# The order of the last loads and of the last products in a one-core decode kernel (attention, gated feed-forward, mixed)

## The chip, the cores and the metric

One core of a Trainium2 chip. The metric is the device time of one execution in microseconds, the median of several runs. Unless marked ns, all times are microseconds from the start of the span.

## The reference

One token `x` of 512 numbers goes through two branches, and a gate mixes them:

```python
q = (x @ wq) as 32 heads of 128          # D = 512
# 8 key heads of 32768 x 128, each shared by 4 query heads
p = softmax(q . k * 128**-0.5)
a = concat_heads(p @ v) @ wo             # wo: 4096 x 512
b = (silu(x @ w1) * (x @ w3)) @ w2       # w1, w3: 512 x 1792, w2: 1792 x 512
g = sigmoid(sum(x * gate_w))
out = g * a + (1 - g) * b                # 512 numbers
```

All is float32. In units of 2^20 bytes, keys and values are 128 MB each, wo and wq 8 MB each, w1, w3 and w2 3.5 MB each; each byte is read once, 296.2 million bytes in all.

## The kernel before, in words

The kernel writes out the order of each engine by hand: a small planner (`Program`) keeps a list of operations per engine and puts a semaphore wait wherever an operation reads or overwrites what another engine or a transfer has written. Nothing is reordered after that. All large loads are issued by SP (`load`, whose DMA is line 191), in the order in which they stand in the program; a load that has to wait for its buffer holds back every load behind it.

Two large buffers of 8 MB, `big_a` and `big_b`, take keys and values. Each has two halves of 4 MB, `region(b, z)`, whose keys in the planner are A0, A1, B0, B1. In the main part, keys come through `big_a` (two early tiles through `big_b`), VectorE transposes them in 32 x 32 blocks, TensorE forms the scores, and values of earlier heads come through `big_b` and are multiplied by the probabilities. The keys of all eight heads and the values of heads 0 to 5 go through this; the part runs to about 600 us.

The end of the kernel, lines 478 to 649, is written out straight:

- `load_halves` and further loads bring the last values, heads 6 and 7 (half-heads 12 to 15), each in one or more pieces. `values` (line 540) multiplies one half buffer, or some of its four groups of 16 blocks, and accumulates in the bank `ps_o`.
- `load_wo(w)` loads a quarter of wo (2 MB) into the one buffer `wo_t`. `mix(w)` (line 527) adds the rows of that quarter on VectorE, eight additions into `acc` [128 partitions x 512], weighted with the attention outputs of heads 2w and 2w + 1. The loads of quarters 1 to 3 therefore each wait for the eighth addition of the quarter before. The fourth quarter isn't mixed on VectorE: its products run on TensorE.
- `last_head(h)` (lines 549 to 556) takes a head's sum out of `ps_o` by four VectorE operations, a product on TensorE (line 555), and a scaling; `place` (lines 509 to 521) spreads the result over the partitions by a multiplication, a product (line 513), a mask and a sum. For the last head the result is `otp`, the weights of the last wo products.
- w2 goes into `region(0, 0)`, 14 row blocks `k` of 512 columns (`w2t[:, k, :]`), in five transfers `parts`: blocks 0 to 3, 4 to 7, 8 to 10, 11 and 12, 13.
- `wide` (line 624) multiplies by blocks 0 to 7 of w2 and by the last wo and accumulates into bank f0 (`pa`) in four groups of 32 partitions. VectorE then adds `pa` to `acc` (line 632). `ff_down` (line 639) accumulates into bank f1 (`pb`): first `ones` times `acc`, the sum over the partitions, then blocks 8 to 13 of w2. `res` is the copy of `pb` (line 647), and ScalarE's queue issues the output.
- `idle_product(n)` (line 606) is a product of n columns whose result nobody reads. It waits for nothing; TensorE, which takes its instructions in order, does it where it stands.

The order of the last loads on SP before: third wo; B0; B1a (2 MB); the wait for `mix(2)`; fourth wo; B1b and B1c (1 MB each); the five parts of w2. The order of TensorE before, from the last values on: values of B0, B1a, B1b; idle 512; values of B1c; idle 512 and 256; last head; `place`; w2 blocks 0 to 3; idle 256; wo; w2 blocks 4 to 7; (VectorE's addition, beside it idle 512); sum of `acc` over partitions; w2 blocks 8 to 13.

A float32 product is two records in the profile, so that "x16" under line 540 or 624 is eight products.

Of the kernel before, what the change touches and what calls it, by code (L numbers as in the profile page):

```python
# [116 lines left out]
def kernel(  # L117
# [14 lines left out]
    _, HKV, S, DH = k_cache.shape  # L132
# [12 lines left out]
    R = NB * DH  # L145
# [3 lines left out]
    FR = F // P  # L149
# [11 lines left out]
    def sbuf(name, *shape):  # L161
        return nc.alloc_sbuf_tensor(name, [P, *shape], F32)[:]

    big = [sbuf("big_a", 2 * R), sbuf("big_b", 2 * R)]
    wo_t = sbuf("wo_t", 8, D)
# [11 lines left out]
    acc = sbuf("acc", 512)  # L177
    otp = sbuf("otp", 8, 32)
    htp = sbuf("htp", FR, 32)
# [7 lines left out]
    def load(dst, src, writes, over=()):  # L187
        lanes[0] += 1
        lane = f"load{lanes[0] % 12}"
        return pr.add(  # L190
            "SP", lambda: nc.sync.dma_start(dst, src), writes=writes, over=[*over, lane], inc=lane, by=16, also=lane,
        )

    def region(b, z):
        return big[b][:, z * R:(z + 1) * R]
# [12 lines left out]
    ident, ones, fold = sbuf("ident", P), sbuf("ones", P), sbuf("fold", 32)  # L208
# [18 lines left out]
    for src, dst, view, axes in (  # L227
# [11 lines left out]
            reads=[src], writes=[dst])  # L239
# [24 lines left out]
    for c in range(NC):  # L264
# [19 lines left out]
        reads=["gate0"], writes=["gate1"])  # L284
# [41 lines left out]
    vd = v_cache.rearrange("a h (e p n) d -> (a h) e p (n d)", e=2, p=P)  # L326
# [155 lines left out]
    def load_wo(w):  # L482
        load(wo_t, wo[w * 8 * P:(w + 1) * 8 * P, :].rearrange("(p k) e -> p k e", k=8), ["wo"])
# [22 lines left out]
    def place(ws, rows, i, over=()):  # L506
        n, w0 = len(ws), ws[0]
        mine = each[i][:, 0:n]
        dve(lambda: V.tensor_mul(
            mine, on[:, 8 * w0:8 * w0 + 8 * n].rearrange("p (w t) -> p w t", w=n).unsqueeze(2).to_broadcast([P, n, 8, 8]),  # L510
            own_k.unsqueeze(1).unsqueeze(3).to_broadcast([P, n, 8, 8]),
        ), reads=["own_k"] + [("on", 2 * w + u) for w in ws for u in range(2)], writes=[f"each{i}"])
        pe(lambda: T.matmul(  # L513
            pm[i][:, 0:64 * n], spot.rearrange("p t x -> p (t x)"), mine.rearrange("p w k t -> p (w k t)"),
            start=True, stop=True,
        ), reads=["spot", f"each{i}"], writes=[f"m{i}"])
        dve(lambda: V.tensor_mul(
            mine, pm[i][:, 0:64 * n].rearrange("p (w k t) -> p w k t", w=n, t=8),
            mask.unsqueeze(1).unsqueeze(1).to_broadcast([P, n, 8, 8]),
        ), reads=[f"m{i}", "mask"], writes=[f"each{i}"])  # L520
        dve(lambda: V.tensor_reduce(rows, mine, axis=AX.X, op=ALU.add),
            reads=[f"each{i}", *over], writes=[("own", w) for w in ws])


    def mix(w):
        for k in range(8):
            dve(lambda k=k: V.scalar_tensor_tensor(  # L527
                acc, wo_t[:, k, :], own_rows[:, w, k:k + 1], acc, op0=ALU.mult, op1=ALU.add,
            ), reads=["wo", ("own", w), "acc"], writes=["acc"])


    def values(h, e, z, vt, key, groups=range(4)):
        u = h % 2

        def go():
            for g in groups:
                for t in range(4):
                    o = 256 * g + 128 * z + 64 * e + 16 * t
                    n = 16 * g + 4 * t
                    ins = T.matmul(  # L540
                        ps_o[32 * t:32 * t + 32, :], prob[u][:, o:o + 32], vt[:, n * P:(n + 4) * P],
                        start=((e, z, g) == (0, 0, 0)), stop=((e, z, g) == (1, 1, 3)),
                    )
            return ins
        pe(go, reads=[key, f"pad{u}", ("prob", u)], writes=["o"])

    def last_head(h):
        r = red[h % 2]
        dve(lambda: V.tensor_scalar(r, ps_o[:, 0:P], own_b[:, 0:1], None, op0=ALU.mult),  # L549
            reads=["o", "own_b"], writes=[("red", h % 2)])  # L550
        for b in range(1, 4):
            dve(lambda b=b: V.scalar_tensor_tensor(
                r, ps_o[:, b * P:(b + 1) * P], own_b[:, b:b + 1], r, op0=ALU.mult, op1=ALU.add,
            ), reads=["o", "own_b", ("red", h % 2)], writes=[("red", h % 2)])
        pe(lambda: T.matmul(pm[1][:, 0:REP], r, own_q, start=True, stop=True), reads=["own_q", ("red", h % 2)], writes=["m1"])
        dve(lambda: V.tensor_mul(on[:, 4 * h:4 * h + 4], pm[1][:, 0:REP], recip[:, 4 * h:4 * h + 4]),
            reads=["m1", ("recip", 3)], writes=[("on", h)])
# [20 lines left out]
    for z in range(2):  # L578
        values(6, 1, z, region(1, z), f"B{z}")
    last_head(6)  # L580
    cuts = (0, R, R + 4096, R + 6144, 2 * R)
    names = ("B0", "B1a", "B1b", "B1c")

    def load_piece(i):
        a, b = cuts[i:i + 2]
        load(big[1][:, a:b], vd[7, 1][:, a:b], [names[i]], over=["B1"] if i else [])

    load_piece(0)
    load_piece(1)
    mix(2)  # L590
    load_wo(3)
    load_piece(2)
    load_piece(3)
    for z in range(2):
        values(7, 0, z, region(0, z), f"A{z}")

# [1 line left out]
    w2t = region(0, 0)[:, 0:FR * D].rearrange("p (k e) -> p k e", k=FR)  # L598
    w2d = w2.rearrange("(p k) e -> p k e", k=FR)
    parts = ((0, 4), (4, 8), (8, 11), (11, 13), (13, 14))  # L600
# [4 lines left out]
    def idle_product(n):  # L605
        pe(lambda: T.matmul(ps_s[:, 0:n], ones, sb[:, 0:4].rearrange("p n i m -> p (n i m)")[:, 0:n], start=True, stop=True),  # L606
           reads=["ones"], writes=["s"])

    values(7, 1, 0, region(1, 0), "B0")
    for n, gs in zip(names[1:], (range(0, 2), range(2, 3), range(3, 4))):  # L610
        if n == "B1c":
            idle_product(512)
        values(7, 1, 1, region(1, 1), n, gs)
    idle_product(512)
    idle_product(256)
    last_head(7)
    place(range(3, 4), otp[:, :, 0].unsqueeze(1), 1, ["otp"])
    pa, pb = pf[0], pf[1]

    def wide(ws, **kw):  # L620
        def go():
            for j, (w, t, first, last) in enumerate(ws):
                r = 32 * (j % 4)
                ins = T.matmul(pa[r:r + 32, :], w, t, start=first, stop=last)  # L624
            return ins
        pe(go, writes=["f0"], **kw)

    wide([(htp[:, k, :], w2t[:, k, :], True, False) for k in range(4)], reads=["htp", ("w2", 0)])
    idle_product(256)
    wide([(otp[:, k, :], wo_t[:, k, :], False, False) for k in range(8)], reads=[("own", 3), "otp", "wo"])  # L630
    wide([(htp[:, k, :], w2t[:, k, :], False, True) for k in range(4, 8)], reads=["htp", ("w2", 4)])
    dve(lambda: V.tensor_add(acc, acc, pa), reads=["acc", "f0"], writes=["acc"])
    idle_product(512)

    def ff_down(ws, **kw):
        def go():
            for w, t, first, last in ws:
                for j in range(4):
                    ins = T.matmul(pb[32 * j:32 * j + 32, 0:P], w, t[:, j * P:(j + 1) * P], start=first, stop=last)  # L639
            return ins  # L640
        pe(go, writes=["f1"], **kw)

    ff_down([(ones[:, 0:32], acc, True, False)], reads=["ones", "acc"])
    for a, b in parts[2:]:
        ff_down([(htp[:, k, :], w2t[:, k, :], False, k == FR - 1) for k in range(a, b)], reads=["htp", ("w2", a)])
    res = sbuf("res", P)
    dve(lambda: V.tensor_copy(res, pb[:, 0:P]), reads=["f1"], writes=["res"])
    pr.add("ACT", lambda: nc.scalar.dma_start(out.rearrange("a b (j e) -> (a b j) e", e=P), res[0:P:32, :]),
           reads=["res"], inc="out", by=16)
# [5 lines left out]
    a = next(i for i, o in enumerate(ops) if o.loop)  # L655
    b = max(i for i, o in enumerate(ops) if o.loop) + 1
# [58 lines left out]
```

## Time and profile before

| | |
|---|---|
| median of 3 runs | 699.58 us (699.52 to 699.82) |
| the profiled execution | 699.89 us |
| its span | 698.1 us |
| bytes read | 296.23 MB, 424 GB/s over the span |
| busy: TensorE, VectorE, ScalarE, GpSimd | 402.4, 376.1, 45.3, 2.6 us |
| mean granted clock of TensorE | 0.78 |

The profile gives, for each engine, the instructions with start and duration; for each transfer the time of its issue on SP and the time until it has landed; and a chain of work that ended last, followed back from the last instruction through what released each step. "PE" is TensorE, "PEld" its loading of weights, "DVE" VectorE, "SPq" the queue that SP issues transfers to. A piece of the chain that is named DMA is time in which the next step waited for that transfer. The clock of TensorE is given as a share of full speed.

### The profile page before, as it was taken

How to read it: one execution, taken by the hardware profiler on the slowest of the kernel's cores; microseconds unless marked ns; L12 is line 12 of the kernel's file. 1: busy time of each engine (PE TensorE's matmuls, PEld its weight loads, DVE VectorE, ACT ScalarE, POOL GpSimd, SP SyncE). 2: the span in 40 equal slices, each digit the busy share in tenths (PEclk: the TensorE clock that was granted, in tenths of full speed). 3: DMA queues.
4: the chain of work that ended last, by engine and by line, in shares of the span. 5: the costliest groups of instructions: out<-in, count | busy, mean ns of one | idle time of the engine just before them, and what ended most of it. 6: DMA issues, size and time to landing. Idle time of an engine off the chain costs nothing. (4 is left out here: it accounts for less than half of the span.)

```text
span 698.1 us, 5677 instructions
## 1 busy us (share of the span) xinstructions
PE 402.4 (58%) x2400; PEld 94.3 (14%) x2400; DVE 376.1 (54%) x263; ACT 45.3 (6%) x90; POOL 2.6 (0%) x15
## 2 busy tenths in 40 slices
PE   3636556656556654647565555656365565267447
PEld 1100101201010101201010101201010101121012
DVE  1029999796619091786528090886437180744301
ACT  0200000011100000020100000020001000100000
POOL 1000000000000000000000000000000000000000
PEclk9866888877887887867667886869877678676768
DMA  9999999999999999999999999999999999999994
GB/s 385 428 430 434 424 441 430 447 419 425 456 411 453 417 432 432 454 407 441 428 432 454 407 441 422 456 412 449 419 428 460 407 449 419 435 419 437 428 419 193
DMA packets 9524, 296.34 MB, mean 425 GB/s; under 512 B 1062, under 2 KB 1066, under 8 KB 1452
## 3 DMA queue, kind: packets, MB, share of 16 engines
q1 hardware_dynamic: 9506, 296.23, 98.6%
q8 instruction: 5, 0.08, 0.0%
q14 instruction: 3, 0.02, 0.0%
q10 hardware_dynamic: 10, 0.00, 0.0%
HBM read 296.23 MB, written 0.00 MB: 424 GB/s over the span
## 5 line engine op out<-in xcount | busy, mean ns | idle before, releaser
L355 DVE STREAM_TRANSPOSE kt<-big_a 128x2048 f32<-128x2048 f32 x112 | 250.3, 2287 | 182.6 <-DMA big_a<-in_A_k_cache_dram 158.4
L344 PE MATMUL ps<-kt,winc 128*32 128x512 f32 x1024 | 183.0, 795 | 132.1 <-PEq L665 131.9
L430 PE MATMUL ps<-big_b,pv 128*32 128x512 f32 x768 | 111.2, 744 | 74.3 <-PEq L665 74.3
L344 PEld LDWEIGHTS ps<-kt,winc 128*32 128x32 f32 x1024 | 26.6, 122 | 284.3 <-issue 284.3
L430 PEld LDWEIGHTS ps<-big_b,pv 128*32 128x32 f32 x768 | 30.6, 133 | 154.6 <-issue 154.6
L355 DVE STREAM_TRANSPOSE kt<-big_b 128x2048 f32<-128x2048 f32 x16 | 35.6, 2283 | 3.3 <-DMA big_b<-in_A_k_cache_dram 2.3
L244 PE MATMUL ps<-acc 128*128 128x512 f32 x34 | 22.2, 740 | 21.8 <-PEq L665 20.2
L527 DVE SCALAR_TENSOR_TENSOR acc<-wo_t,own_rows,acc 128x512 f32<-128x512 f32 x24 | 18.0, 752 | 28.5 <-DMA wo_t<-in_A_wo_dram 27.8
L540 PE MATMUL ps<-big_b,probs 128*32 128x512 f32 x128 | 20.3, 791 | 20.4 <-DMA big_b<-in_A_v_cache_dram 20.4
L338 ACT COPY winc<-win 128x128 f32<-128x128 f32 x32 | 9.8, 306 | 338.3 <-PE ps L344 338.2
L361 ACT COPY sb<-ps 128x512 f32<-128x512 f32 x16 | 17.0, 1063 | 152.9 <-PE ps L344 152.9
L540 PE MATMUL ps<-big_a,probs 128*32 128x512 f32 x128 | 19.2, 759 | 5.5 <-DMA big_a<-in_A_v_cache_dram 5.5
L403 DVE TENSOR_REDUCE sums<-probs 128x8 f32<-128x2048 f32 x4 | 15.3, 3815 | 8.0 <-ACT probs L398 8.0
L442 DVE TENSOR_TENSOR tmp<-ps,own_b 128x512 f32<-128x512 f32 x12 | 7.9, 656 | 19.8 <-PE ps L430 19.8
L307 PE MATMUL turned<-big_b,xp 128*32 128x448 f32 x64 | 10.5, 826 | 8.2 <-DMA big_b<-in_B_w_dram 8.2
L270 PE MATMUL turned<-big_a,xp 128*32 128x512 f32 x64 | 11.2, 861 | 3.1 <-DMA big_a<-in_A_wq_dram 2.9
L549 DVE TENSOR_SCALAR red<-ps,own_b 128x128 f32<-128x128 f32 x2 | 0.7, 348 | 21.3 <-PE ps L540 21.3
L446 DVE TENSOR_REDUCE red<-tmp 128x128 f32<-128x1024 f32 x6 | 11.5, 1917 | 0.2
L244 PEld LDWEIGHTS ps<-acc 128*128 128x128 f32 x34 | 5.7, 210 | 38.3 <-issue 36.7
L398 ACT ACTIVATE probs<-turned 128x1024 f32<-128x1024 f32 x8 | 7.8, 1020 | 38.5 <-DVE turned L393 38.5
L393 DVE TENSOR_TENSOR turned<-turned,top 128x2048 f32<-128x2048 f32 x4 | 9.2, 2300 | 0.1
L540 PEld LDWEIGHTS ps<-big_b,probs 128*32 128x32 f32 x128 | 4.4, 137 | 35.9 <-DMA big_b<-in_A_v_cache_dram 23.8
(80 smaller groups left out, 102.2 us busy)
## 6 DMA issues: line engine op xcount, KB each, us to landing
big_a<-in_A_k_cache_dram SPq DMA_DIRECT2D x28, 4096.0 KB, 28.5
big_b<-in_A_k_cache_dram SPq DMA_DIRECT2D x4, 4096.0 KB, 30.9
big_a<-in_A_v_cache_dram SPq DMA_DIRECT2D x4, 4096.0 KB, 28.0
big_a<-in_A_wq_dram SPq DMA_DIRECT2D x2, 4096.0 KB, 16.6
wo_t<-in_A_wo_dram SPq DMA_DIRECT2D x4, 2048.0 KB, 15.6
big_b<-in_B_w_dram SPq DMA_DIRECT2D x2, 3584.0 KB, 33.8
big_b<-in_A_v_cache_dram SPq DMA_DIRECT2D x1, 4096.0 KB, 27.3
big_b<-in_A_v_cache_dram SPq DMA_DIRECT2D x1, 2048.0 KB, 31.8
```

Source lines behind the costliest of these rows:

```text
L244: return T.matmul(ps_s, acc[:, 0:P], acc, start=True, stop=False, skip_group_check=True)
L270: ins = T.matmul(pf[b][32 * j:32 * j + 32, :], xp[:, c, :], t[:, o:o + REP * DH], start=(c == 0), stop=(c == NC - 1),)
L307: ins = T.matmul(pf[2 + z][32 * j:32 * j + 32, 0:FJ], xp[:, c, :], t[:, o:o + FJ], start=(c == 0), stop=(c == NC - 1),)
L338: lambda: A.copy(winc, win[:, t // 4, :, 16 - 16 * z:48 - 16 * z]),
L344: ins = T.matmul(ps_s[32 * g:32 * g + 32, :], winc[:, c, :], kt[c % 2][:, 512 * g:512 * g + 512], start=False, stop=False, skip_group_chec ...
L355: k = dve(lambda c=c, d=dst: V.transpose(d, kin[:, c]), reads=[key], writes=[f"kt{c % 2}"], credit="keys")
L361: lambda: A.copy(sb[:, :, :, t % 4], ps_s.rearrange("p (n i) -> p n i", i=32)),
L403: dve(lambda: V.tensor_reduce(sums[:, 8 * w:8 * w + 8].rearrange("p (u q) -> p u q", u=2), probs[:, :, 0:1024].rearrange("p u (n q) -> p u ...
L430: ins = T.matmul(ps_o[32 * t:32 * t + 32, :], pv[:, o:o + 32], big[1][:, n * P:(n + 4) * P], start=((z, g) == (0, 0)), stop=((z, g) == (1, ...
L446: dve(lambda: V.tensor_reduce(red[h], tmp.rearrange("p e b d -> p d (e b)"), axis=AX.X, op=ALU.add), reads=["tmp0", "tmp1"], writes=[("red ...
L527: dve(lambda k=k: V.scalar_tensor_tensor(acc, wo_t[:, k, :], own_rows[:, w, k:k + 1], acc, op0=ALU.mult, op1=ALU.add,), reads=["wo", ("own ...
L540: ins = T.matmul(ps_o[32 * t:32 * t + 32, :], prob[u][:, o:o + 32], vt[:, n * P:(n + 4) * P], start=((e, z, g) == (0, 0, 0)), stop=((e, z, ...
```

## The change

On SP, the second half of B1 is one transfer of 2 MB in place of two of 1 MB, and is issued directly behind B1a; the fourth wo comes behind it, and then w2 as before. The values of head 7 so come in three pieces (B0, B1a, B1b), and the fourth wo behind all of them.

On TensorE, the order from the last values on is: values of B0, B1a; idle 512 twice; values of B1b (two groups); idle 512; the last head's product, with an idle 256 between it and `place`; wo, which now starts the accumulation in `pa`; idle 512; w2 blocks 0 to 3 and 4 to 7; then, in `pb`, w2 blocks 8 to 10; the sum of `acc` over partitions; blocks 11 and 12; block 13. So the sum over partitions stands behind eleven row blocks of w2 instead of eight.

```diff
-    cuts = (0, R, R + 4096, R + 6144, 2 * R)
-    names = ("B0", "B1a", "B1b", "B1c")
-
-    def load_piece(i):
-        a, b = cuts[i:i + 2]
-        load(big[1][:, a:b], vd[7, 1][:, a:b], [names[i]], over=["B1"] if i else [])
-
-    load_piece(0)
-    load_piece(1)
+    cuts = (0, R, R + 4096, 2 * R)
+    names = ("B0", "B1a", "B1b")
+    for (a, b), n in zip(zip(cuts, cuts[1:]), names):
+        load(big[1][:, a:b], vd[7, 1][:, a:b], [n], over=[] if n == "B0" else ["B1"])
     mix(2)
     load_wo(3)
-    load_piece(2)
-    load_piece(3)
     for z in range(2):
         values(7, 0, z, region(0, z), f"A{z}")
...
     values(7, 1, 0, region(1, 0), "B0")
-    for n, gs in zip(names[1:], (range(0, 2), range(2, 3), range(3, 4))):
-        if n == "B1c":
-            idle_product(512)
-        values(7, 1, 1, region(1, 1), n, gs)
+    values(7, 1, 1, region(1, 1), "B1a", range(2))
+    for _ in range(2):
+        idle_product(512)
+    values(7, 1, 1, region(1, 1), "B1b", range(2, 4))
     idle_product(512)
+    last_head(7)
     idle_product(256)
-    last_head(7)
     place(range(3, 4), otp[:, :, 0].unsqueeze(1), 1, ["otp"])
...
-    wide([(htp[:, k, :], w2t[:, k, :], True, False) for k in range(4)], reads=["htp", ("w2", 0)])
-    idle_product(256)
-    wide([(otp[:, k, :], wo_t[:, k, :], False, False) for k in range(8)], reads=[("own", 3), "otp", "wo"])
-    wide([(htp[:, k, :], w2t[:, k, :], False, True) for k in range(4, 8)], reads=["htp", ("w2", 4)])
+    wide([(otp[:, k, :], wo_t[:, k, :], k < 4, False) for k in range(8)], reads=[("own", 3), "otp", "wo"])
+    idle_product(512)
+    for a, b in parts[:2]:
+        wide([(htp[:, k, :], w2t[:, k, :], False, k >= 4) for k in range(a, b)], reads=["htp", ("w2", a)])
     dve(lambda: V.tensor_add(acc, acc, pa), reads=["acc", "f0"], writes=["acc"])
-    idle_product(512)
...
-    ff_down([(ones[:, 0:32], acc, True, False)], reads=["ones", "acc"])
     for a, b in parts[2:]:
-        ff_down([(htp[:, k, :], w2t[:, k, :], False, k == FR - 1) for k in range(a, b)], reads=["htp", ("w2", a)])
+        ff_down([(htp[:, k, :], w2t[:, k, :], k == 8, k == FR - 1) for k in range(a, b)], reads=["htp", ("w2", a)])
+        if a == 8:
+            ff_down([(ones[:, 0:32], acc, False, False)], reads=["ones", "acc"])
```

In the changed kernel the lines behind the loads stand seven lines earlier, up to nine at the end: the products of `wide` are line 617, of `ff_down` line 631, the idle products line 599, VectorE's addition line 625, the copy to `res` line 640.

## The prediction

> **What bounds the kernel now.** I read the page first (span, slices, queues), then the chain that ended last, then SP's timeline and the list of DMA issues in the last 60 us, and last the TensorE clock by windows.
>
> ```profile
> span 698.1 us, 5677 instructions
> DMA  9999999999999999999999999999999999999994
> ```
>
> The DMA engines are full in 39 of 40 slices and not in the last: up to there the stream from memory sets the time, behind it something else does. The chain, from the last transfer in it to the last instruction that computes:
>
> ```profile
> 664.02 15.28 DMA big_b<-in_A_v_cache_dram
> 679.30 0.04 issue
> 679.35 1.94 PE ps L540 x8
> 681.28 2.00 PE ps L606 x2
> 683.29 1.63 PE ps L540 x8
> ...
> 686.51 0.40 PE ps L555 x2
> ...
> 687.41 0.43 PE ps L513 x2
> 687.84 0.99 PE turned L624 x8
> 688.84 0.63 PE ps L606 x2
> 689.47 2.71 PE turned L624 x24
> 692.18 1.06 PE ps L606 x2
> 693.23 1.71 PE turned L639 x56
> 694.97 0.29 DVE res L647
> ```
>
> From the landing of the value piece B1b at 679.30 on, the chain is TensorE and VectorE alone: the last value products, the last head, the wo products (L624), the w2 products (L624 and L639), the result. No w2 transfer is in it. Were they there long before? SP's timeline (start, duration) and the DMA issues by group (count, size, us from issue to landing; a landing below is issue plus that figure):
>
> ```profile
> 639.33 0.33 SPq L191 DMA_DIRECT2D wo_t<-in_A_wo_dram  x1
> 639.70 0.91 SPq L191 DMA_DIRECT2D big_b<-in_A_v_cache_dram  x2
> 663.65 0.33 SPq L191 DMA_DIRECT2D wo_t<-in_A_wo_dram  x1
> 664.97 2.65 SPq L191 DMA_DIRECT2D big_a<-in_B_w_dram  x5
> ```
>
> ```profile
> big_b<-in_A_v_cache_dram SPq DMA_DIRECT2D x1, 4096.0 KB, 27.3
> big_b<-in_A_v_cache_dram SPq DMA_DIRECT2D x1, 2048.0 KB, 31.8
> wo_t<-in_A_wo_dram SPq DMA_DIRECT2D x1, 2048.0 KB, 13.2
> big_a<-in_B_w_dram SPq DMA_DIRECT2D x2, 1024.0 KB, 20.3
> big_a<-in_B_w_dram SPq DMA_DIRECT2D x1, 768.0 KB, 22.7
> big_a<-in_B_w_dram SPq DMA_DIRECT2D x1, 512.0 KB, 23.5
> big_a<-in_B_w_dram SPq DMA_DIRECT2D x1, 256.0 KB, 23.6
> ```
>
> ```profile
> L191 SPq DMA_DIRECT2D big_a<-in_B_w_dram x1: 752/752/752, 666.9 to 666.9; - x1
> ```
>
> So B0 lands at 639.70 + 27.3 = 667.0, B1a at 640.2 + 31.8 = 672.0, the last wo at 663.65 + 13.2 = 676.85, B1b at 679.30; the first two w2 pieces at 665.2 + 20.3 = 685.5 on average, 1 MB apart, so 684.3 and 686.7; the next three, issued at about 665.9, 666.4 and 666.9, at 688.6, 689.9 and 690.5. They land in the order of issue, and 2 MB of distance is 4.85 us each time: one stream, served in turn. It is done at 690.5, and the result is copied out at 694.97. That gap of 4.5 us is all that a change of the end can win.
>
> **The change part by part.** *The order of the loads.* The second half of B1 (2 MB) goes out as one transfer right behind B1a, at about 640.6, and no longer behind the last wo. It needs the same buffer as B1a, so it brings no wait of its own; SP has nothing else to do until 663.65, where the eighth addition of the third wo frees wo_t. The third wo is issued ahead of all these (639.33), so that time stays. The last wo is issued at 663.65 as before, 13 us ahead of its place in the stream, and the five w2 loads queue behind it on SP, now 0.95 us earlier; neither matters while the stream serves in turn. What changes is that place: B1b takes that of the last wo (676.85), and wo takes that of B1b and B1c, 4.9 us later, at 681.75. Every w2 piece has the same bytes ahead of it, so its landing stays: the last at 690.5. One transfer less to start and to complete is worth nothing here, at least not more than the scatter of the times before (0.3 us).
>
> *The values.* The price of 16 records at full clock, of a DVE hand-over, and of a short group, by the timeline:
>
> ```profile
> 667.09 7.17 PE L540 MATMUL ps<-big_b,probs 128*32 128x512 f32 x48 [9.27 <-DMA big_b<-in_A_v_cache_dram]
> ```
>
> ```profile
> 671.98 0.12 PEld L540 LDWEIGHTS ps<-big_b,probs 128*32 128x32 f32 x4 [0.35 <-DMA big_b<-in_A_v_cache_dram]
> ```
>
> ```profile
> 688.14 0.22 DVE L521 TENSOR_REDUCE otp<-each 128x8 f32<-128x64 f32 x1
> 692.25 0.69 DVE L632 TENSOR_TENSOR acc<-acc,turned 128x512 f32<-128x512 f32 x1 [3.89 <-PE turned L624]
> ```
>
> ```profile
> 693.16 0.43 PE L639 MATMUL turned<-acc,ones 128*32 128x128 f32 x8
> ```
>
> B1a's 16 records run from 671.98 to 674.26, 2.28 us. Two idle products of 512 columns (1.06 each, as at 692.18) follow, to 676.4; then a pause of 0.5 us until B1b is there. Does the clock survive that? The windows (last three figures: granted clock, DMA share, GB/s):
>
> ```profile
> 667.00:670.00 3.00, 2.91 (x16) 0.79 (x20) 0.00 (x0) 0.00 (x0) 0.00 (x0) 0.50 1.00 426
> 671.00:674.50 3.50, 3.26 (x32) 0.73 (x24) 0.00 (x0) 0.00 (x0) 0.00 (x0) 1.00 0.95 405
> 674.50:679.30 4.80, 0.00 (x0) 0.00 (x0) 0.00 (x0) 0.00 (x0) 0.00 (x0) 0.82 1.01 418
> 679.30:684.00 4.70, 4.65 (x14) 0.91 (x18) 0.00 (x0) 0.00 (x0) 0.00 (x0) 0.50 1.01 422
> 685.00:688.00 3.00, 2.33 (x12) 1.23 (x15) 1.86 (x7) 0.00 (x0) 0.00 (x0) 1.00 1.00 406
> 690.00:690.50 0.50, 0.50 (x12) 0.13 (x4) 0.00 (x0) 0.00 (x0) 0.00 (x0) 1.00 0.00 0
> ```
>
> In the pause of 4.8 us the clock was still full for most of the time (mean 0.82), and then half for the 4.7 us behind it, which is why 8 records cost 1.94 and an idle product 2.00 in the chain. A pause of a tenth of that should keep it: I take full clock, and keep the half-clock price for the range. So the values end at 676.9 + 2.3 = 679.2, where before they ended at 684.92 (the chain): 2.45 us from the earlier landing, the rest from the clock and from the idle product that stood ahead of B1c.
>
> *The last head.* From the end of the values (683.29 + 1.63) to otp it was 684.92 to 688.36, 3.44 us; the idle product of 256 columns (0.63) now stands between the head's product and the next one. The head's product ends 1.99 us behind the values (686.91), the idle one at 2.62, where the next product could start at 2.49: 0.1 us on the path. otp is there at 682.75, one us behind wo (681.75). The idle 512 ahead of it (1.06) lies beside the 1.59 us of DVE ahead of the head's product.
>
> *wo and w2.* Off the path come 0.99 + 0.63 us (w2's first block and an idle product ahead of wo). By the chain a record of L624 is 2.71/24 = 0.113 us, one of L639 1.71/56 = 0.0305. wo: 16 records, 1.8, to 684.6; idle 512, 1.06, to 685.65; w2 rows 0 to 3, landed, 0.9, to 686.55; rows 4 to 7 land at 686.7, 0.9, to 687.65, whereupon DVE adds (0.69) until 688.4, beside a wait of TensorE for rows 8 to 10 (688.6). These are 24 records, 0.73, to 689.35; the sum of acc over partitions, 8 records, 0.25, to 689.6. It is no longer ahead of the L639 products, and DVE's 0.69 is hidden in full. Rows 11 and 12 land at 689.9, 0.5 to 690.4; row 13 at 690.5, 0.04 to start (679.30 to 679.35) and 0.43 for a group of 8: 690.97. **res is copied at 691.0 instead of 694.97: 3.97 us.** Behind it (copy, output, end) nothing changes. Without the waits for landings the same sum ends at 689.3, so TensorE's part has 1.7 us to spare, and the stream is what ends last.
>
> That a landing needs 0.5 us at most behind the last bytes is read from the last window row: nothing moves from 690.0 on, and row 13 lands at 690.5. [...]
>
> The profiled execution took 699.89 us, 1.79 beside its span, and the median is 699.58. Taken off the median: 699.58 - 3.97 = 695.6.
>
> **Rivals.** *Half clock to the end (slower).* TensorE now stands still in many short pauses: 0.5 ahead of B1b, 0.5 to 0.6 at each hand-over, 0.9 ahead of row 8, 0.3 ahead of row 11. If these sum up to a fallback of the clock at B1b, by the chain's rows at half clock: values 1.94 + 1.71, to 680.55; idle product 2.0, to 682.55; head's product 0.8, idle 256 1.26, place 0.86 and 0.52 of DVE, to 686.0; wo 3.6, idle 2.1, w2 3.6, to 695.3; then 56 records 3.4, to 698.75: 3.8 us later than 694.97, **703.4**. It decides late: half clock delays by 9.5 us in all, of which 1.7 are spare and 4.0 are the gain, so it must last through the idle product behind wo. Against it: from 685 to 688 of the trace TensorE was idle 0.67 us in 3, at a clock of 1.00, and continuous work brought the clock back within 6 us both times. [...] 4%. A fall that lasts only 5 us, as after 679.35, costs 2.5 less the 1.7 spare: 696.4, inside the forecast.
>
> *Transfers in flight share the stream (slower).* If the three value pieces were served side by side, all would land when their 8 MB are through, at 676.85; then B0's and B1a's 48 records (7.17, half of it cold) and 16 more (1.8) end at 685.85, and the 10.1 us that the rest takes without waits end at 695.95: 1.0 later, **700.6**. It decides from a common landing at 675.9 on. Against it: B0 and B1a, in flight together for 27 us, landed 5 us apart. [...] 4%.
>
> *The stream ends later.* The end now follows the last landing one for one, and before it had 4.5 us of cover. A rate 2% lower over the last 50 us is 1 us; no change would need 8%. With 2 to 4 us: **697.6 to 699.6**. The rates of the windows (405 to 426 GB/s with a full stream) speak for less than that. 4%, half of it inside 0.2%.
>
> **How the numbers follow.** The forecast has 88%. Its range: down to 695.1, if the last landing is at 690.0, where the bytes end; up to 697.1, for 5 us of half clock (696.4) and a stream 0.7 us later together. A measurement of this kernel tells about 0.2%, 1.4 us, from no change; the likeliest gain is almost three times that. Faster: 88% and half of the late stream, 90%; same 2%; slower 4 + 4 = 8%.
>
> **What would show it.** Right: B1b lands near 676.9 and the last wo near 681.8; no PE row at half clock between 676 and 691; the values end near 679.2; L631 (L639 before) waits for the w2 transfers; the chain ends in a DMA of w2, and res is copied within 0.6 us of row 13's landing. Wrong: a last landing later than 691; the wait of the wo product ending on the DMA of wo rather than on DVE; B1b landing beside B1a; cold groups behind B1b; a chain that still runs through TensorE and VectorE alone from 677 on.

## The result, and the profile after

The changed kernel takes 696.16 us (median of 6 runs, 695.86 to 696.39), the kernel before 699.83 us in the same session (699.52 to 700.33). The ratio is 0.9947 with a 95% interval of 0.9934 to 0.9960: faster by 3.7 us where 4.0 were forecast, and inside the range. The profiled execution has a span of 694.0 us, 4.1 less than before; at 695.86 us it is the shortest of the six, which is one reason why the profile shows a little more than the medians.

The chain that ended last in the changed kernel, from the end of the third mix on, where SP can issue the fourth wo (start, duration, what):

```profile
663.48 0.02 issue
663.49 0.33 SPq L191
...
665.25 0.04 issue
665.29 24.38 DMA big_a<-in_B_w_dram
689.67 0.04 issue
689.71 1.11 PE turned L631 x24
690.82 0.02 issue
690.85 0.29 DVE res L640
```

Before, this stretch of the chain held a DMA of values until 679.30 and then 15.6 us of TensorE and VectorE. Now one transfer of w2 (the fourth of five, blocks 11 and 12) covers 24.4 us of it, and 1.2 us are left behind its landing. The stream sets the end.

From SP's timeline, the last issues (start, duration), and behind them the transfers issued after 655 us (size, us from issue to landing):

```profile
639.56 1.38 SPq L191 DMA_DIRECT2D big_b<-in_A_v_cache_dram  x3
663.49 0.33 SPq L191 DMA_DIRECT2D wo_t<-in_A_wo_dram  x1
663.87 2.33 SPq L191 DMA_DIRECT2D big_a<-in_B_w_dram  x5
```

```profile
wo_t<-in_A_wo_dram SPq DMA_DIRECT2D x1, 2048.0 KB, 18.1
big_a<-in_B_w_dram SPq DMA_DIRECT2D x2, 1024.0 KB, 22.2
big_a<-in_B_w_dram SPq DMA_DIRECT2D x1, 768.0 KB, 23.6
big_a<-in_B_w_dram SPq DMA_DIRECT2D x1, 512.0 KB, 24.4
big_a<-in_B_w_dram SPq DMA_DIRECT2D x1, 256.0 KB, 24.5
```

The last wo now takes 18.1 us instead of 13.2 from its issue, because B1b is ahead of it: it lands at 681.6. The last piece of w2, issued at about 665.75, lands at 690.25, where before it was 690.5. TensorE's timeline between B1b and the last products:

```profile
676.73 1.92 PE L540 MATMUL ps<-big_b,probs 128*32 128x512 f32 x16 [0.35 <-DMA big_b<-in_A_v_cache_dram]
682.20 1.92 PE L617 MATMUL turned<-wo_t,otp 128*32 128x512 f32 x16 [0.57 <-DVE otp L521]
686.58 1.06 PE L617 MATMUL turned<-big_a,htp 128*32 128x512 f32 x8 [0.40 <-DMA big_a<-in_B_w_dram]
688.48 0.86 PE L631 MATMUL turned<-big_a,htp 128*32 128x128 f32 x24 [0.83 <-DMA big_a<-in_B_w_dram]
```

B1b's products start at 676.73; the wo product waits for otp on VectorE, not for wo; the w2 products wait for their transfers, 0.40 and 0.83 us. The granted clock (third figure from the end) in three windows of this stretch:

```profile
677.00:680.00 3.00, 2.71 (x18) 0.56 (x10) 1.17 (x4) 0.00 (x0) 0.00 (x0) 1.00 0.93 396
680.00:683.00 3.00, 2.13 (x14) 1.10 (x18) 1.07 (x5) 0.00 (x0) 0.00 (x0) 1.00 1.00 418
686.00:688.00 2.00, 1.24 (x12) 0.16 (x8) 0.29 (x1) 0.00 (x0) 0.00 (x0) 1.00 1.00 398
```

It is full, also where TensorE was busy for 1.24 us of 2 only.

### The profile page after: what moved, and what is told of

Its sections match the earlier page's. It is cut to its first block, busy times and chain, and to the rows that moved or that the text cites. A ratio compares the mean times of both kernels' runs of the same rounds, so it can differ in the third digit from the quotient of the medians.

```text
span 694.0 us, 5676 instructions
## 1 busy us (share of the span) xinstructions
PE 402.1 (58%) x2400; PEld 92.6 (13%) x2400; DVE 376.2 (54%) x263; ACT 45.3 (7%) x90; POOL 2.6 (0%) x15
## 5 line engine op out<-in xcount | busy, mean ns | idle before, releaser
L344 PE MATMUL ps<-kt,winc 128*32 128x512 f32 x1024 | 186.1, 807 | 132.7 <-PEq L658 132.7
L244 PE MATMUL ps<-acc 128*128 128x512 f32 x34 | 20.5, 687 | 21.8 <-PEq L658 20.3
L540 PE MATMUL ps<-big_a,probs 128*32 128x512 f32 x128 | 20.7, 811 | 5.1 <-DMA big_a<-in_A_v_cache_dram 5.1
L381 DVE TENSOR_REDUCE mt<-turned 128x8 f32<-128x2048 f32 x4 | 9.0, 2260 | 0.0
```

Of the source, the lines that this page charges most:

```text
L244: return T.matmul(ps_s, acc[:, 0:P], acc, start=True, stop=False, skip_group_check=True)
L344: ins = T.matmul(ps_s[32 * g:32 * g + 32, :], winc[:, c, :], kt[c % 2][:, 512 * g:512 * g + 512], start=False, stop=False, skip_group_chec ...
L540: ins = T.matmul(ps_o[32 * t:32 * t + 32, :], prob[u][:, o:o + 32], vt[:, n * P:(n + 4) * P], start=((e, z, g) == (0, 0, 0)), stop=((e, z, ...
```

## The experiments

The theory: B1b's place in the stream brings the gain, TensorE's part has 1.7 us to spare, and the last landing of w2 ends the time. The rivals: the gain lies in TensorE's order; it lies in the earlier issue of B1b; TensorE's chain still ends last. Each kernel of the experiments was timed against the kernel before, which had medians of 699.4 to 700.2 us in these sessions; the ratio is to the kernel before of the same session. "After" below is the changed kernel. The edits are shown shortened ("..."), and against after where nothing else is said.

The executions reach the end of the kernel at slightly different times. The last column therefore counts from one mark, the issue on SP that waits for the third mix (the fourth wo; in "B1b issued late" B1b itself). It lies at 663.65 before, 663.49 in after and between 663.59 and 663.89 in the others. From this mark the products of B1b start 13.22 to 13.28 us later in every kernel with the new order of loads, so the mark fits the stream.

| | ratio to before (95%) | res copied at | res, from the mark |
|---|---|---|---|
| before | 1 | 694.97 | 31.32 |
| after | 0.9947 (0.9934 to 0.9960) | 690.85 | 27.36 |
| loads alone | 0.9978 (0.9969 to 0.9987) | 694.31 | 30.43 |
| loads alone, clock held | 0.9956 (0.9942 to 0.9969) | 691.45 | 27.80 |
| TensorE's order alone | 1.0012 (0.9987 to 1.0037) | 694.57 | 30.74 |
| TensorE's order alone, clock held | 0.9980 (0.9971 to 0.9989) | 693.29 | 29.58 |
| before, clock held | 0.9983 (0.9973 to 0.9992) | 693.01 | 29.36 |
| B1b issued late | 0.9947 (0.9934 to 0.9960) | 691.02 | 27.34 |
| no idle products | 0.9952 (0.9939 to 0.9965) | 691.56 | 27.77 |
| two products later | 0.9953 (0.9939 to 0.9966) | 691.08 | 27.32 |
| six products later | 1.0005 (0.9996 to 1.0014) | 694.32 | 30.68 |
| 1 MB of w2 less | 0.9917 (0.9903 to 0.9930) | 688.75 | 24.86 |
| sum first | 0.9950 (0.9936 to 0.9963) | 690.94 | 27.35 |

**The loads alone.** After's loads, TensorE's order of before (with one idle product ahead of B1b):

```diff
-    wide(... wo ...); idle_product(512)
-    for a, b in parts[:2]: wide(... w2 rows a to b ...)
+    wide(... w2 rows 0 to 3 ...); idle_product(256)
+    wide(... wo ...); wide(... w2 rows 4 to 7 ...)
...
+    idle_product(512)
+    ff_down(... ones, acc ...)
     for a, b in parts[2:]: ff_down(... w2 ...)
```

> The order of loads of the changed kernel with TensorE's order of before (w2's first block ahead of wo, the sum over partitions ahead of blocks 8 to 13). Theory (place in the stream): the values end near 678.7, the head near 682.1, then w2's first block waits for its landing (684.0), wo ends near 687.5, block group 4 to 7 at 688.4, VectorE's addition at 689.2, all of L639's products by 691.4: res about 0.6 us later than in the changed kernel, 3.0 to 3.5 us faster than before. Rival (the gain is TensorE's order): little of the gain is left, under 1.5 us faster than before.

Faster by 0.22%, some 1.5 us: neither the 3.0 to 3.5 of the theory nor clearly the rival. TensorE's timeline and the clock of the profiled execution show why:

```profile
684.50 1.93 PE L616 MATMUL turned<-big_a,htp 128*32 128x512 f32 x8 [2.49 <-DMA big_a<-in_B_w_dram]
687.52 3.14 PE L616 MATMUL turned<-wo_t,otp 128*32 128x512 f32 x16
```

```profile
680.00:683.00 3.00, 1.35 (x7) 0.72 (x5) 1.42 (x6) 0.00 (x0) 0.00 (x0) 1.00 1.01 423
683.00:686.00 3.00, 1.50 (x8) 0.20 (x8) 0.00 (x0) 0.00 (x0) 0.00 (x0) 0.53 0.98 408
686.00:688.00 2.00, 2.00 (x10) 0.70 (x10) 0.00 (x0) 0.00 (x0) 0.00 (x0) 0.50 1.00 400
```

With w2's first block ahead of wo, TensorE waits 2.49 us for it, and the clock is lost there: 8 records cost 1.93 instead of 1.06, the 16 of wo 3.14 instead of 1.92. That was in none of the expectations. The profiled execution, 699.35 us, is the longest of eleven: eight took 698.0 to 698.4 us and three 699.0 to 699.4, so it shows about 1 us more loss than the median. Two idle products in this wait, ahead of the first block, test it (the edit is against the loads alone):

```diff
+    for _ in range(2):
+        idle_product(512)
     wide(... w2 rows 0 to 3 ...)
```

> The loads of the changed kernel with TensorE's order of before, and two idle products of 512 columns in the pause of 2.5 us that TensorE had ahead of w2's first block (681.99 to 684.50). Theory (what that kernel lacked was the clock, lost in that pause): the products behind it run at full clock, block 0 to 3 at 685.5, wo ends near 687.9, res near 691.6, that is 0.75 us later than in the changed kernel and about 2.9 us faster than before; 1.5 to 2 us faster than without the two idle products. Rival (TensorE's order of before costs by itself): not over 0.5 us faster than without them.

```profile
684.26 1.06 PE L616 MATMUL turned<-big_a,htp 128*32 128x512 f32 x8 [0.71 <-DMA big_a<-in_B_w_dram]
685.88 1.92 PE L616 MATMUL turned<-wo_t,otp 128*32 128x512 f32 x16
```

Full clock, res at 691.45 (691.6 expected), and 696.34 us against 698.19 without the two products (ratios to before 0.9956 and 0.9978; by the medians 1.85 us, within the 1.5 to 2 expected). What held the loads alone back was the clock, not TensorE's order by itself; that costs 0.6 us of res against after, 0.4 counted from the mark.

**TensorE's order alone.** The loads of before, all else as in after:

```diff
-    load(... B0, B1a, B1b ...)
+    load_piece(0); load_piece(1)
     mix(2)
     load_wo(3)
+    load_piece(2); load_piece(3)
...
-    values(7, 1, 1, region(1, 1), "B1b", range(2, 4))
+    for n, gs in (("B1b", range(2, 3)), ("B1c", range(3, 4))):
+        values(7, 1, 1, region(1, 1), n, gs)
```

> The loads of before (the last wo ahead of B1b and B1c) with TensorE's order of the changed kernel. Theory (place in the stream): B1b lands at 679.3, B1c at 681.8, the values end near 682.9, otp is there at 686.4, wo ends at 688.2, idle 689.3, blocks 0 to 7 at 691.1, the rest at 693.1: 1.9 us faster than before at full clock, 2.2 us slower than the changed kernel; with the clock at half behind the pause ahead of B1b some 1 us faster than before. Rival (the gain is TensorE's order): 3 us or more faster than before.

No difference from before that can be told; three of its twelve executions took 701.8 to 709.3 us, which makes the interval wide. The rival's 3 us or more is excluded. The theory had 1.9 us for a full clock and some 1 us for a half clock; the profile shows 0.4 (0.6 from the mark). The windows:

```profile
677.00:680.00 3.00, 0.84 (x5) 0.16 (x8) 0.00 (x0) 0.00 (x0) 0.00 (x0) 0.98 1.00 418
680.00:683.00 3.00, 2.19 (x16) 0.20 (x8) 0.00 (x0) 0.00 (x0) 0.00 (x0) 0.50 1.00 418
683.00:686.00 3.00, 3.00 (x12) 0.91 (x5) 1.40 (x4) 0.00 (x0) 0.00 (x0) 0.50 1.01 419
```

The clock falls here too, though TensorE stood still for only 2.16 us ahead of B1b and was at work again when it fell. With two more idle products in that pause and one between B1b and B1c (the edit is against TensorE's order alone):

```diff
-    for _ in range(2):
+    for _ in range(4):
         idle_product(512)
...
+        if n == "B1c":
+            idle_product(512)
```

> The loads of before with TensorE's order of the changed kernel, and three more idle products of 512 columns: two in the pause of 2.2 us ahead of B1b, one between B1b and B1c. Theory (with B1c at 682.0 the values can't end before 683.1, and the clock was lost ahead of B1c): full clock throughout, otp near 686.6, res near 693.35, some 1.6 us faster than before and 2.5 us slower than the changed kernel. Rival (clock isn't what kept this order from its gain): same time as without the three, no gain over before.

res at 693.29 (693.35 expected), faster than before by 0.20%. The clock stayed full. What is left is B1c, whose products don't start ahead of about 681.9 with these loads, in either order of TensorE.

**The kernel before, clock held.** How much of that is the clock alone? The edit is against the kernel before:

```diff
-        if n == "B1c":
-            idle_product(512)
+        for _ in range({"B1a": 0, "B1b": 4, "B1c": 1}[n]):
+            idle_product(512)
```

> The kernel before with four idle products of 512 columns in the pause of 4 to 5 us ahead of B1b, nothing else changed. Theory (part of the gain of the change is the clock alone): B1b and B1c at full clock, values end near 683.1 instead of 684.9, and the 10.05 us behind them as before: res at 693.15, 1.8 us faster than before. So the clock would carry about 1.8 of the 3.9 us, the order of the loads the rest. Rival (the whole gain is the order of the loads): no difference to before.

```profile
679.36 1.06 PE L540 MATMUL ps<-big_b,probs 128*32 128x512 f32 x8 [1.16 <-DMA big_b<-in_A_v_cache_dram]
681.85 1.06 PE L540 MATMUL ps<-big_b,probs 128*32 128x512 f32 x8 [0.37 <-DMA big_b<-in_A_v_cache_dram]
```

B1b's and B1c's products cost 1.06 each instead of 1.94 and 1.63; res is at 693.01 (693.15 expected) and the time is 0.17% below before, 1.2 us (by the medians 1.6). Against the kernel above with the order of after and the same loads, 693.29: with a held clock TensorE's order brings nothing on these loads.

**B1b issued late.** After's order of the stream, but B1b is issued only behind the third mix (naming "acc" makes its load wait for that):

```diff
     load_piece(0); load_piece(1)
     mix(2)
+    load(big[1][:, cuts[2]:cuts[3]], ..., ["B1b"], over=["B1", "acc"])
     load_wo(3)
```

> The changed kernel, with B1b issued only behind the third mix (663.5), directly ahead of the last wo: the same order of the stream, 23 us later on SP. Theory (only the place in the stream counts): B1b lands at 676.7 as in the changed kernel, time within 0.3 us of it. Rival (it is the early issue that counts, a transfer issued late starts late): B1b lands at 679 or later and the time is 2 us or more above the changed kernel.

B1b's products start at 676.91 (676.73 in after; from the mark 13.23 and 13.24), the ratio is that of after. The place counts; 23 us of earlier issue count for nothing.

**No idle products.** All five are left out of after's end:

```diff
-    for _ in range(2):
-        idle_product(512)
     values(7, 1, 1, region(1, 1), "B1b", range(2, 4))
-    idle_product(512)
     last_head(7)
-    idle_product(256)
...
-    idle_product(512)
```

> The changed kernel without the idle products of its end (two ahead of B1b, one behind the values, one ahead of place, one behind wo). TensorE then stands still for 2.3 us ahead of B1b and for 1.6 us behind the values. Theory: the products have 1.7 us to spare and the end is set by the last landing of w2; even if the clock fell for a few us, the time is within 0.5 us of the changed kernel. Rival (half clock to the end): 4 to 7 us slower than the changed kernel.

```profile
677.02 2.98 PE L540 MATMUL ps<-big_b,probs 128*32 128x512 f32 x16 [2.63 <-DMA big_b<-in_A_v_cache_dram]
683.99 3.64 PE L613 MATMUL turned<-wo_t,otp 128*32 128x512 f32 x16 [0.57 <-DVE otp L521]
```

```profile
680.00:683.00 3.00, 0.87 (x5) 0.78 (x4) 1.79 (x6) 0.00 (x0) 0.00 (x0) 0.50 0.99 415
686.00:688.00 2.00, 2.00 (x12) 0.39 (x8) 0.00 (x0) 0.00 (x0) 0.00 (x0) 0.50 1.01 402
688.00:690.00 2.00, 2.00 (x40) 0.92 (x32) 0.33 (x1) 0.00 (x0) 0.00 (x0) 1.00 0.36 141
```

The clock is at half from 677.7, just behind the start of B1b's products, to 688.0, and still res is only 0.7 us later, 0.4 from the mark: what TensorE has to spare, and the idle products that no longer stand on its path, swallow most of it. The intervals of the two overlap.

**TensorE later by two and by six idle products**, behind wo:

```diff
-    idle_product(512)
+    for _ in range(3):   # 7 in the second kernel
+        idle_product(512)
```

> The changed kernel with two more idle products of 512 columns behind wo (2 x 1.06 = 2.1 us of TensorE on the way to w2's products). Theory (TensorE has 1.7 us to spare, the last landing ends the time): at most 0.2 to 0.4 us slower than the changed kernel. Rival (TensorE's chain is still what ends last): 2.1 us slower.

> The changed kernel with six more idle products of 512 columns behind wo (6.4 us). Theory: the 1.7 us to spare are used up and the rest shows, 4.5 us slower than the changed kernel, about the time of before or 0.5 us above it. Rival (TensorE's chain ends last without anything to spare): 6.4 us slower.

With two more, res is 0.2 us later, and not at all later from the mark (27.32 and 27.36). With six more, the chain runs through TensorE again:

```profile
684.30 6.21 PE ps L599 x14
690.50 1.90 PE turned L617 x16
```

Seven products take 6.21 us where one took 1.06, so 5.15 were added, not the 6.4 expected. res is 3.47 later than in after, 3.32 from the mark. The difference, 1.68 us, or 1.83 from the mark, is what TensorE had to spare; 1.7 was the prediction's figure.

**Less stream.** Blocks 0 to 3 of w2 are neither loaded nor multiplied:

```diff
-    for a, b in parts:
+    for a, b in parts[1:]:
         load(w2t[:, a:b, :], ...)
-    for a, b in parts[:2]:
+    for a, b in parts[1:2]:
         wide(...)
```

> The changed kernel without row blocks 0 to 3 of w2: neither loaded (1 MB less of the stream) nor multiplied (8 records, 0.9 us of TensorE less); the output lacks their part. Theory (the stream ends last): all later landings are 2.45 us earlier, the last near 687.8, and as TensorE's part has 1.7 us and now 0.9 more to spare, the time is 2.3 to 2.5 us below the changed kernel. Rival (TensorE's chain): 0.9 us below it.

0.9917 against 0.9947 for after: 0.30%, 2.1 us, as is the difference in res. From the mark it is 2.50 us, and by the median spans (694.25 and 691.8) 2.45: the 2.45 us of the stream, and far over the 0.9 us of TensorE's work left out. The chain of this profile runs through VectorE's addition again, so TensorE's part and the stream end almost together; but res still comes about 0.6 us behind the last landing, as in after.

**The sum first.** The sum of `acc` over partitions ahead of blocks 8 to 13:

```diff
+    ff_down(... ones, acc ...)
     for a, b in parts[2:]:
         ff_down(... w2 ...)
-        if a == 8:
-            ff_down(... ones, acc ...)
```

> The changed kernel with the sum of acc over partitions ahead of row blocks 8 to 13, as before, instead of behind blocks 8 to 10. Theory: VectorE's addition ends at 688.4, where blocks 8 to 10 land; the sum (0.25 us) then pushes them to 689.4, still ahead of the landing of blocks 11 and 12 (689.7): within 0.2 us of the changed kernel. Rival (the place of the sum matters): 0.7 us or more slower.

res at 690.94 against 690.85 (27.35 and 27.36 from the mark), and ratios that can't be told apart. Where the sum stands is worth nothing measurable here.

## Why the prediction was right, point by point

*The place in the stream.* Landings in the order of issue, wo 4.9 us later, w2 where it was: shown by the issue rows, and by the late issue of B1b, which changes nothing. The last landing came 0.2 us earlier than taken over from before, but the mark did too (663.49 and 663.65): counted from it, the landing stayed to 0.1 us. That also bears on the two transfers of 1 MB that became one of 2 MB, which no run tests by itself: the same bytes took the same time.

*The values and the head.* They were to end at 679.2; VectorE took them over at 678.73. A group of 16 records is 1.92 us rather than the 2.28 read off B1a's, which had begun while B0's products were still running. otp was to be there at 682.75, was at 682.14. 0.16 us of each difference is the earlier mark. Both errors lie in what TensorE has to spare and didn't reach the end.

*The end.* res at 691.0, measured 690.85. Against the forecast gain of 3.97 us, the profile shows 4.12 at this place, 3.96 counted from the mark, and the medians of one session 3.67. The forecast of 695.6 was taken off a median of 699.58; the six runs before of that session gave 699.83. The remaining 0.3 us are inside the interval, so that 3.96 and 3.97 agree so closely is luck.

*To spare.* 1.7 us, measured 1.68, or 1.83 from the mark. That it fits so closely is partly luck: counted from the mark, otp came 0.45 us earlier than forecast, and behind it TensorE and VectorE without waits take some 6.9 us to res where the sum had 6.55.

*The clock.* It stayed full, as assumed, but for another reason than the one given. The prediction held a pause of 0.5 us to be harmless because one of 4.8 us had cost the clock only late. In TensorE's order alone a pause of 2.16 us was enough. The clock fell 1.2 us into the last pause of the loads alone and 3.4 us into the pause of before, so the time since the start of a pause doesn't decide by itself. What does wasn't shown; the last section has what TensorE did ahead of each fall, and after's figures beside it.

*The rivals.* Half clock to the end didn't come: it is the idle products that prevent it (without them the windows show 0.50 from 678 to 688, with them 1.00), and in three of the kernels above the clock fell. That short pauses sum up, as that rival supposed, would fit the fall in the loads alone, 1.2 us into a pause and behind 3 us with 1.35 us of TensorE's work; no run tests it. Its price wasn't tested as it was stated, since its sum counts the idle products at half clock too; in the kernel without them the clock was at half for some 10 us, and the time hardly moved. Transfers side by side: refuted by B1b at 676.7 behind B1a at 671.8. A later end of the stream: it came no later.

*What the argument lacked.* It put the gain down to the earlier landing and, in passing, to the clock. By the ratios, the held clock alone is worth 1.2 us on the loads before (1.6 by the medians), and the new order of the loads without a held clock about 1.5; together they give 3.1 (loads alone, clock held), and 3.7 with TensorE's order of after. That last step of 0.6 us is the least certain: the two intervals overlap, and from the mark it is 0.4. So the runs fit that TensorE's new order matters mostly because wo's products, and the idle one behind them, fill the time until w2's first block is there, which keeps the clock; which of the two does it wasn't tested.

## What to carry to other kernels

At the end of a kernel that is bound by its stream, sort the last loads by the work that hangs behind each: the piece with the longest chain behind it first, the pieces whose products are short and independent last, until the last landing itself ends the chain. Then see what the engine does while it waits: a new wait ahead of a product can cost the clock, and the loads' gain with it. In the loads alone the wait of 2.49 us did (a mean clock of 0.53 from 683 to 686), and the two idle products that held it were worth 1.85 us by the medians. From 680 to 683 TensorE was busy there for 1.35 us, and in after, which kept the clock, for 2.13. Whether a step of the end is worth anything can be read off beforehand: sum the chain without waits for transfers, and what lies below the last landing is free.

## What the runs showed of the hardware that wasn't expected

The clock of TensorE fell at pauses of 2.16 us (TensorE's order alone), 2.49 us (the loads alone) and 2.63 us (no idle products), in the first and the last of these after TensorE had begun to work again. In the loads alone, in finer windows of the same kernel (TensorE's busy time, clock, DMA share, GB/s):

```profile
682.50:683.00 0.50, 0.00 (x0) 1.00 1.10 459
683.00:683.50 0.50, 0.00 (x0) 0.70 0.86 360
683.50:684.00 0.50, 0.00 (x0) 0.50 1.18 492
```

it fell at about 683.2, 1.2 us into the pause, behind a stretch from 680 on in which TensorE was busy for 1.35 us of 3. After's TensorE was busy for 2.13 us of the same 3 and kept it.

The other two falls, in windows of the same kind, first TensorE's order alone and then no idle products:

```profile
679.50:680.00 0.50, 0.46 (x4) 0.86 1.06 442
680.00:680.50 0.50, 0.50 (x8) 0.50 0.98 410
```

```profile
677.50:678.00 0.50, 0.50 (x8) 0.75 0.69 295
678.00:678.50 0.50, 0.50 (x8) 0.50 1.07 459
```

By the means the clock fell at about 679.9, 0.3 us behind the start of B1b's products (679.54), and at about 677.7, 0.7 us behind it (677.02). In the first kernel TensorE had been busy for 0.84 us of the 3 from 677 to 680, in the second for none of the 2.5 from 674.5 to 677.

The kernel before fell from full clock at 677.62, 3.4 us into the pause that begins at 674.26, and was back at 684.45. After's clock was full with TensorE busy for 1.24 us of the 2 from 686 to 688, and that of TensorE's order alone with the clock held with 0.58 us of the 2 from 678 to 680, in which a pause of 1.81 us ends. So a pause that had lasted 1.2 us was enough in one kernel and 1.81 us were not in another: the time that TensorE has stood still doesn't tell by itself whether the clock falls. What sets the time of a fall, and how busy TensorE has to be, wasn't shown. The busy times are the profile's, in which ends of products are modelled. The loads alone have two groups of times; whether the clock makes them wasn't shown either, since only one of the executions was traced.

Idle products of 512 columns in a row are cheaper than one alone: 0.89 us each of seven (6.21 us together, in the kernel with six more), 1.06 for one (at 692.18 in the kernel before).
